# Three stretches of a fused attention and GELU kernel with their instructions put in another order

## The chip, the cores and the metric

The kernel runs on one core of a Trainium2 chip. The metric is the device time of one execution in microseconds (us). The engines work side by side, each through its own queue in order: TensorE (PE; its weight loads are listed apart as PEld), VectorE (DVE), ScalarE (ACT), GpSimd (POOL) and SyncE (SP), which issues the DMAs.

## The reference

A polynomial-sketch attention makes x, and a two-layer block with exact GELU is applied to x. Everything is float32 in the end (some inputs arrive as 64-bit words, and the kernel makes float32 of them itself).

```python
# q, k, v: (4, 4, 1088, 32); S1, S2: (8, 32); w_in: (128, 2048); w_out: (2048, 128)
def phi(x):
    a = np.einsum('rd,bhsd->bhsr', S1, x)
    b = np.einsum('rd,bhsd->bhsr', S2, x)
    return np.einsum('bhsi,bhsj->bhsij', a, b).reshape(*x.shape[:-1], r * r)
q_p, k_p = (phi(q), phi(k))
kv = np.einsum('bhsf,bhsd->bhfd', k_p, v)
z = np.sum(k_p, axis=2)
num = np.einsum('bhsf,bhfd->bhsd', q_p, kv)
den = np.einsum('bhsf,bhf->bhs', q_p, z)[..., None] + 1e-06
attn = num / den
x = attn.transpose(0, 2, 1, 3).reshape(B * S, H * D)      # 4352 tokens x 128
h = x @ w_in
g = 0.5 * h * (1.0 + erf(h / sqrt(2)))
out = g @ w_out
```

## The kernel before

**Tiles.** The 1088 tokens of each of the 4 batches are cut into two chunks of 512 and a rest of 64. That gives 8 main chunks (n = 0 to 7, two for each batch) and a ninth, the remainder, that holds the rests of all four batches, 256 tokens wide. For each chunk an x of 128 channels by tokens (xT) is made, and then 16 blocks (fi) of 128 hidden channels are gone through: `hidden(n, fi)` multiplies w_in by xT into a PSUM bank (L683) and ScalarE applies GELU (L690). For chunks 0 and 1 the first 8 blocks go through `project` (L818), an ordinary product with w_out that adds up in one PSUM bank. All other main blocks go through `two_products` (L767), a Strassen-like scheme in which GpSimd makes sums of GELU outputs (`token_sums`, L732 to L735) and seven products replace eight. The remainder goes through `project` with tokens as the output's rows (L815).

**Order.** It is written out by hand: at the end of the kernel every instruction is tied behind the one before it on its engine, in the order of the text. Steps t run over (n, fi); at each step come `drain`, then `hidden`, then the lists `slots[t]`, `done[t]` and `products[t]`. The lists hold small pieces of other work that are due at that step: keys and queries of the next batches, weights, the products of blocks whose GELU is done. The products of step (n, fi) are due two steps later (LAG = 2). Step 128 is the remainder's first.

**Prologue.** Before the first step, the keys of batch 0 are turned by TensorE (L333), multiplied with the sketch matrices (L373) and spread into features; key-value sums follow (L417, L423), then the numerators and denominators by token of chunk 0 (`numerators_by_token`, L635). `keep_busy` (L848) puts matmuls of zeros ahead of all this: 3 of 256 columns at the start, one of 128 columns later. A float32 matmul goes through TensorE in two passes, so each shows as two records.

**From numerator to x.** `divide` (L642) does three things on VectorE: it adds 1e-6 to the denominators (L650), takes the reciprocal (L651) and multiplies (L656) into x_tok, tokens by channels. For chunk 0 this is done in two halves of the tokens, the first with its products in two banks h_ps, the second in two banks o_ps. `turn_half` (L660) turns 256 tokens by two transposes on TensorE (L664) into a PSUM bank, and a copy (L665) brings it to xT: the first half by ScalarE, the second by VectorE. `first_hidden` (L697) then does the first hidden product by halves of the tokens.

**Chunk 1** goes the same way at step t = 3, beside chunk 0's first hidden blocks: numerators (L635, 64 records), `divide` in one piece, then the products `project(0, 0)` and `project(0, 1)`, and at step t = 4 the two turns with their copies, the first half of the first hidden product, `project(0, 2)`, and the second half.

**Weights** arrive as 64-bit words and become float32 in several short instructions (`Rounding`): low words (L260) and exponents (L279) on ScalarE, fields (L268, L273), mantissas (L287), signs (L292) and the product (L297) on VectorE. For the second piece of w_out, which `project(0, 2)` is the first to read, the mantissas are made by ScalarE and GpSimd (L284, L285); its product L297 on VectorE stands between chunk 1's division and the copy of chunk 1's second half. GpSimd goes on from L285 to `spread_sketches` (L468 to L478), small operations and copies.

**The remainder** gets its x at the end of step 127 by `attend` (L617) with a copy by ScalarE (L623); `products[128]` are four of the products of chunk 7's third block.

Of the kernel before, what the change touches and what calls it, by code (L numbers as in the profile page):

```python
# [8 lines left out]
FP = mybir.dt.float32  # L9
U32 = mybir.dt.uint32  # L10
AX = mybir.AluOpType
ACT = mybir.ActivationFunctionType
# [4 lines left out]
def kernel(  # L17
# [18 lines left out]
    pe, dve, act, pool, sp = nc.tensor, nc.vector, nc.scalar, nc.gpsimd, nc.sync  # L36
    B, H, S, D = q.shape
# [4 lines left out]
    NF = d_ff // 128  # L42
    NP = H // 2
# [3 lines left out]
    JC = 4  # L47
# [3 lines left out]
    C = D + 1  # L51
    LAG = 2
    NMAIN = B * NCH
# [7 lines left out]
    att = ctx.enter_context(tc.tile_pool(name="att", bufs=2))  # L61
# [9 lines left out]
    def work_bank():  # L71
        return work_banks()[:, 0]
# [11 lines left out]
    by_act, by_dve, by_pool = act.copy, dve.tensor_copy, pool.tensor_copy  # L84
# [10 lines left out]
    w_out_sb = [big.tile([128, c1 - c0], FP, name=f"w_out{i}") for i, (c0, c1) in enumerate(pieces)]  # L95
# [428 lines left out]
    def expand_products(n):  # L524


        W = width[n]
        for i in range(2):
            B_of[n, i] = work_banks()
        for s in range(2):  # L530
            for g in range(G):
                for c in range(NP):
                    rows = slice(g * D, (g + 1) * D)
                    pe.matmul(B_of[n, g // 2][c * F:(c + 1) * F, g % 2, s * W // 2:(s + 1) * W // 2],  # L534
                              lhsT=Srep[rows, s].rearrange("p i j -> p (i j)"),
                              rhs=qT[n][rows, 2 * c:2 * c + 2].rearrange("p r j t -> p r (j t)"), start=True, stop=True)
        qp[n] = att.tile([128, 2, CW], FP, name="q_pT")
# [89 lines left out]
    def numerators_by_token(n, banks, tokens):  # L627

        for at, i in enumerate(tokens):
            for r in range(2):  # L630
                for half in range(2):
                    for c in range(NP):
                        rows, col, tok = slice(c * F, (c + 1) * F), (at * 2 + r) * C, i * 128 + half * 64
                        v_at = r * 2 * D
                        pe.matmul(banks[c][half * 64:(half + 1) * 64, col:col + C], lhsT=qp[n][rows, r, tok:tok + 64],  # L635
                                  rhs=kz[0][rows, v_at:v_at + C], start=True, stop=True)
# [2 lines left out]
        x_tok[n, i] = att.tile([128, 2, H, D], FP, name=f"x_tok{i}", bufs=1)  # L639
        return x_tok[n, i]  # L640

    def divide(n, banks, tokens, by_head_pair):  # L642

        g = len(tokens) * 2
        den = att.tile([128, NP, JC * 2], FP, name="den_tok")[:, :, :g]
        parts = [slice(c, c + 1) for c in range(NP)] if by_head_pair else [slice(0, NP)]
        nd = [(banks[c.start][:, None] if by_head_pair else banks)[:, :, :g * C].rearrange("p b (g c) -> p b g c", c=C)
              for c in parts]
        for c, x in zip(parts, nd):
            dve.tensor_scalar(out=den[:, c], in0=x[:, :, :, D], scalar1=1e-6, scalar2=None, op0=AX.add)  # L650
        dve.reciprocal(out=den, in_=den)  # L651
        for i in range(len(tokens) // 2):
            to = x_half(n, tokens[0] // 2 + i).rearrange("p j (c r) d -> p c j r d", c=NP)
            for c, x in zip(parts, nd):
                for b in range(c.stop - c.start):
                    dve.tensor_mul(out=to[:, c.start + b], in0=x[:, b, i * 4:i * 4 + 4, 0:D].rearrange("p (j r) d -> p j r d", r=2),  # L656
                                   in1=den[:, c.start + b, i * 4:i * 4 + 4].rearrange("p (j r) -> p j r", r=2)[:, :, :, None]
                                   .broadcast_to([128, 2, 2, D]))

    def turn_half(n, i, ps, copy):  # L660
        if i == 0:
            xT[n] = att.tile([128, CW], FP, name="xT", bufs=3)
        for j in range(2):
            pe.transpose(ps[:, j * 128:(j + 1) * 128], in_=x_tok[n, i][:, j].rearrange("p h d -> p (h d)"), identity=ident)  # L664
        copy(out=xT[n][:, i * 256:(i + 1) * 256], in_=ps[:, :256])  # L665


    g_of, o_of = {}, {}

    def w_tile(w, fi):  # L670
        i = max(i for i, (c0, c1) in enumerate(pieces) if c0 <= fi * 128)
        at = fi * 128 - CUTS[i]
        return w[i][:, at:at + 128]
# [98 lines left out]
    def drain(n):  # L772


        C, N = (att.tile([128, 2, CW], FP, name="sums") for i in range(2))
        lo, hi, one, two = slice(0, 64), slice(64, 128), slice(0, HW), slice(HW, CW)
        a0, a1 = acc[n]

        act.copy(out=C[lo, 0], in_=a1[hi])
        act.copy(out=N[hi, 0, one], in_=C[lo, 0, one])  # L780

        dve.tensor_copy(out=N[lo, 0, one], in_=a0[lo, one])  # L782
        dve.tensor_add(out=C[lo, 1], in0=a1[lo], in1=C[lo, 0])
        dve.tensor_add(out=N[lo, 1, one], in0=a0[lo, two], in1=N[lo, 0, one])
        for half in (lo, hi):
            dve.tensor_add(out=C[half, 0, one], in0=a0[lo, one], in1=C[lo, 1, two])
        dve.tensor_add(out=C[hi, 0, two], in0=a0[hi, two], in1=C[hi, 0, one])
        dve.tensor_add(out=N[hi, 1, one], in0=a0[hi, one], in1=C[hi, 0, two])
        drained[n] = C, N
# [14 lines left out]
            dve.tensor_add(out=N[:, 1], in0=N[:, 1], in1=usual[n])  # L804
        return N[:, 1]

    def project(n, fi, parts=range(B // 2)):
        first, final = fi == 0, fi == (USUAL if n < NCH else NF) - 1
        if first:
            o_of[n] = out_bank() if n < NMAIN else [work_bank() for i in range(B // 2)]  # L810
        g = g_of[n, fi]
        if n == NMAIN:

            for i in parts:
                pe.matmul(o_of[n][i][:, :128], lhsT=g[:, i * 128:(i + 1) * 128], rhs=w_tile(w_out_sb, fi),  # L815
                          start=first, stop=final)
            return
        pe.matmul(o_of[n], lhsT=w_tile(w_out_sb, fi), rhs=g, start=first, stop=final)  # L818

    def store(n):  # L820
        oT = mlp.tile([128, JC, d_model], FP, name="oT")
# [23 lines left out]
    def keep_busy(n, ps, cols=256):  # L845
        for i in range(n):
            noughts = [nc.const_aps.tensor(0.0, [128, m], FP) for m in (128, cols)]
            pe.matmul(ps[:, CW - cols:], lhsT=noughts[0], rhs=noughts[1], start=True, stop=True)  # L848

    bank = work_bank()  # L850
    keep_busy(3, bank)
    r = Rounding(SR)
    r.low_words()
    r.fields()
# [10 lines left out]
    banks = [out_bank(), out_bank()]  # L865
# [28 lines left out]
    by_act(**late[0])  # L894
    w_in[1].low_words()
    w_in[1].exponent_fields()
    w_in[1].exponents()
    parts = [range(2), range(2, JC)]
    nd = [[hidden_bank(), hidden_bank()], [out_bank(), out_bank()]]
    for banks, tokens in zip(nd, parts):  # L900
        numerators_by_token(0, banks, tokens)
    expand_products(1)
    for banks, tokens in zip(nd, parts):
        divide(0, banks, tokens, by_head_pair=True)
    w_in[1].mantissa_fields()
    turn_half(0, 0, hidden_bank(), by_act)
    turn_half(0, 1, hidden_bank(), by_dve)
# [175 lines left out]
    for t in range(len(steps) + LAG):  # L1083
        if t < 4:

            hidden(0, t)
            if t == 1:
                w_out[0].low_words()
                w_out[0].exponents()
                w_out[0].finish()  # L1090
                w_out[1].fields()
            if t == 2:
                w_out[1].low_words()
            if t == 3:
                banks = work_banks()
                numerators_by_token(1, halves(banks), range(JC))
                w_out[1].mantissas(by_pool=True)
                w_out[1].exponents()
                divide(1, banks, range(JC), by_head_pair=False)
                w_out[1].signs()  # L1100
                w_out[1].product()
                for u in range(4):
                    for f, *a in products[u]:
                        f(*a)
            continue
        if t == 4:
            for i, copy in enumerate((by_act, by_dve)):
                turn_half(1, i, work_bank(), copy)
            first_hidden(1, 0)
            for f, *a in products[t]:  # L1110
                f(*a)
            first_hidden(1, 1)
        for n in drains[t]:
            drain(n)
        if t < len(steps):
            n, fi = steps[t]
            hidden(n, fi, by_halves=t >= 18 and (n < NMAIN or fi < 5))
        if t < len(steps) and steps[t][0] < NMAIN and steps[t][1] % NB == NB - 1:
            n, b = steps[t][0], steps[t][1] // NB
            if b >= first_block(n):  # L1120
                token_sums(n, b)
        for f in slots[t]:
            f()
        for n in done[t]:
            store(n)
        if t != 4:
            for f, *a in products[t]:
                f(*a)
    for n in done[len(steps) + LAG]:
# [40 lines left out]
```

## Time and profile before

| | |
|---|---|
| median of 3 runs | 261.31 us (261.14 to 261.8) |
| profiled execution, its own time | 263.36 us |
| its span, first to last instruction | 261.6 us |
| instructions | 5751 |
| DMA | 13.48 MB, mean 52 GB/s |
| hidden products L683, all | 137.3 us busy in 514 records |
| block products L767, the largest group | 57.5 us busy in 224 records |
| GELU on ScalarE L690 | 73.0 us busy in 128 records |
| sums on GpSimd L732 to L735 | some 36 us each, 28 records each |
| output products L818 | 16.3 us busy in 32 records |

The profile holds one execution of the program, with the start and the length of each instruction. A row such as "L683 PE MATMUL h_ps<-xT,w_in" names the line of the code, the engine, the operation, and which tile is made from which. The matmuls are pipelined: a row's length holds the time that the last results need to leave the array, so the starts of neighbours, and not the lengths, tell how fast they follow each other. Idle time of an engine is put down to the instruction whose semaphore came last.

### The profile page before, as it was taken

How to read it: one execution, taken by the hardware profiler on the slowest of the kernel's cores; microseconds unless marked ns; L12 is line 12 of the kernel's file. 1: busy time of each engine (PE TensorE's matmuls, PEld its weight loads, DVE VectorE, ACT ScalarE, POOL GpSimd, SP SyncE). 2: the span in 40 equal slices, each digit the busy share in tenths (PEclk: the TensorE clock that was granted, in tenths of full speed). 3: DMA queues.
4: the chain of work that ended last, by engine and by line, in shares of the span. 5: the costliest groups of instructions: out<-in, count | busy, mean ns of one | idle time of the engine just before them, and what ended most of it. 6: DMA issues, size and time to landing. Idle time of an engine off the chain costs nothing.

```text
span 261.6 us, 5751 instructions
## 1 busy us (share of the span) xinstructions
PE 256.9 (98%) x2331; PEld 134.7 (51%) x2331; DVE 151.4 (58%) x315; ACT 114.8 (44%) x219; POOL 163.8 (63%) x173
## 2 busy tenths in 40 slices
PE   8999999999999999999999999999999999999994
PEld 6755444344454554444444454444445444445794
DVE  2687678977789997690087957540565043600330
ACT  3465767442535333353335333523453334334441
POOL 3313004799978875687758767787768776877200
PEclk9999999999999999999999999999999999999999
DMA  6449848721000201102000001010001100010020
GB/s 203 136 143 358 218 111 212 217 70 15 0 3 5 33 6 23 20 3 40 3 0 3 0 16 27 4 31 10 3 0 21 21 4 0 12 31 0 3 40 20
DMA packets 29530, 13.48 MB, mean 52 GB/s; under 512 B 21824, under 2 KB 27712, under 8 KB 29504
## 3 DMA queue, kind: packets, MB, share of 16 engines
q1 hardware_dynamic: 29472, 13.12, 20.2%
q8 instruction: 18, 0.29, 0.5%
q14 instruction: 8, 0.07, 0.1%
q10 hardware_dynamic: 32, 0.00, 0.0%
HBM read 10.88 MB, written 2.23 MB: 50 GB/s over the span
## 4 chain that ended last, share of the span: by engine, by line
PE 97%; DVE 1%; issue 0%; ACT 0%
PE h_ps L683 44%; PE o_ps L767 33%; PE o_ps L818 5%; PE w_ps L815 3%; PE w_ps L428 1%; PE w_ps L617 1%; PE w_ps L568 1%; PE w_ps L848 1%; PE h_ps L697 1%; PE h_ps L333 1%; PE o_ps L417 1%; PE w_ps L534 1%; PE w_ps L934 1%; PE w_ps L635 0%; PE o_ps L373 0%; DVE x_tok L656 0%
## 5 line engine op out<-in xcount | busy, mean ns | idle before, releaser
L683 PE MATMUL h_ps<-xT,w_in 128*64 128x512 f32 (+3 forms) x514 | 137.3, 576 | 0.0
L690 ACT ACTIVATE block<-h_ps 128x512 f32<-128x512 f32 (+1 forms) x128 | 73.0, 571 | 120.5 <-PE h_ps L683 120.1
L767 PE MATMUL o_ps<-block,w_out 128*64 128x256 f32 x224 | 57.5, 379 | 0.0
L683 PEld LDWEIGHTS h_ps<-xT,w_in 128*64 128x64 f32 (+1 forms) x514 | 41.8, 142 | 29.5 <-issue 11.6
L732 POOL TENSOR_TENSOR bits_low<-block 128x512 f32<-128x512 f32 x28 | 35.7, 1274 | 27.5 <-ACT block L690 27.5
L767 PEld LDWEIGHTS o_ps<-block,w_out 128*64 128x64 f32 x224 | 30.5, 137 | 37.5 <-issue 26.7
L733 POOL TENSOR_TENSOR bits_a<-block 128x512 f32<-128x512 f32 x28 | 35.9, 1284 | 12.8 <-ACT block L690 12.8
L734 POOL TENSOR_TENSOR bits_e<-bits_a,block 128x512 f32<-128x512 f32 x28 | 36.1, 1289 | 2.2
L735 POOL TENSOR_TENSOR bits_m<-block,bits_e 128x512 f32<-128x512 f32 x28 | 35.8, 1280 | 2.2
L580 DVE STREAM_TRANSPOSE w_ps<-w_ps 128x512 f32<-128x512 f32 (+1 forms) x7 | 4.9, 693 | 42.7 <-PE w_ps L568 30.0
L767 PE MATMUL o_ps<-block,small 128*64 128x256 f32 x112 | 29.0, 381 | 0.0
L767 PE MATMUL o_ps<-bits_low,small 128*64 128x256 f32 x112 | 29.0, 381 | 0.0
L767 PE MATMUL o_ps<-bits_a,small 128*64 128x256 f32 x112 | 28.8, 379 | 0.0
L767 PE MATMUL o_ps<-bits_m,w_out 128*64 128x256 f32 x112 | 28.7, 379 | 0.0
L767 PEld LDWEIGHTS o_ps<-block,small 128*64 128x64 f32 x112 | 14.9, 137 | 17.7 <-issue 10.1
L782 DVE COPY sums<-o_ps 64x256 f32<-64x256 f32 x8 | 3.3, 417 | 34.6 <-PE o_ps L767 34.6
L767 PE MATMUL o_ps<-bits_e,small 128*64 128x256 f32 x112 | 17.2, 384 | 0.0
L818 PE MATMUL o_ps<-g,w_out 128*128 128x512 f32 x32 | 16.3, 597 | 0.0
L767 PEld LDWEIGHTS o_ps<-bits_m,w_out 128*64 128x64 f32 x112 | 15.3, 137 | 0.0
L767 PEld LDWEIGHTS o_ps<-bits_a,small 128*64 128x64 f32 x112 | 15.2, 137 | 0.0
L767 PEld LDWEIGHTS o_ps<-bits_low,small 128*64 128x64 f32 x112 | 14.9, 137 | 0.0
L767 PEld LDWEIGHTS o_ps<-bits_e,small 128*64 128x64 f32 x112 | 7.5, 136 | 10.6 <-issue 9.1
(181 smaller groups left out, 304.8 us busy)
## 6 DMA issues: line engine op xcount, KB each, us to landing
out_dram<-oT SPq DMA_DIRECT2D x26, 64.0 KB, 2.2
block<-in_moe_w_in_dram SPq DMA_DIRECT2D x3, 512.0 KB, 6.8
block<-in_moe_w_out_dram SPq DMA_DIRECT2D x3, 512.0 KB, 12.3
k<-in_k_dram SPq DMA_DIRECT2D x12, 128.0 KB, 2.8
v<-in_v_dram SPq DMA_DIRECT2D x12, 128.0 KB, 3.3
q<-in_q_dram SPq DMA_DIRECT2D x24, 64.0 KB, 2.2
k<-in_k_dram SPq DMA_DIRECT2D x2, 256.0 KB, 2.9
q<-in_q_dram SPq DMA_DIRECT2D x2, 256.0 KB, 3.8
```

Source lines behind the costliest of these rows:

```text
L333: pe.transpose(ps[:, i * 128:(i + 1) * 128], in_=s, identity=ident)
L580: dve.transpose(out=tok, in_=ps[:, :, :H2])
L683: pe.matmul(ps[rows, :W], lhsT=w[:, rows], rhs=xT[n][:, :W], start=True, stop=True)
L690: act.activation(out=g_of[n, fi][:, :W], in_=ps[:, :W], func=ACT.Gelu)
L732: pool.tensor_sub(out=s[3], in0=a11, in1=a21)
L733: pool.tensor_add(out=s[1], in0=a21, in1=a22)
L734: pool.tensor_sub(out=s[2], in0=s[1], in1=a11)
L735: pool.tensor_sub(out=s[4], in0=a12, in1=s[2])
L767: pe.matmul(acc[n][bank][half * 64:(half + 1) * 64, col:col + HW], lhsT=fixed, rhs=moving, start=opens and e == 0 and name in "4715", stop ...
L782: dve.tensor_copy(out=N[lo, 0, one], in_=a0[lo, one])
L815: pe.matmul(o_of[n][i][:, :128], lhsT=g[:, i * 128:(i + 1) * 128], rhs=w_tile(w_out_sb, fi), start=first, stop=final)
L818: pe.matmul(o_of[n], lhsT=w_tile(w_out_sb, fi), rhs=g, start=first, stop=final)
```

## The change

It has four edits.

1. For the second half of chunk 0's tokens, the addition of 1e-6 moves from VectorE (two L650) to ScalarE: a new function `denominators` does two activations with a bias into the same kind of tile, and `divide` takes it as given. On ScalarE they stand ahead of the exponents (L279) of the second piece of w_in, which move behind them.
2. At step 3, `project(0, 1)` is cut into two halves of its columns, and the two turns of chunk 1 move ahead from step 4 to stand one behind each half; the order of the copies on ScalarE and VectorE stays.
3. At step 128 the list `products[128]` comes ahead of the remainder's first `hidden`.
4. At the start, a fourth `keep_busy` matmul of 64 columns is put behind the three of 256.

```diff
-    def divide(n, banks, tokens, by_head_pair):
+    def divide(n, banks, tokens, by_head_pair, den=None):
         g = len(tokens) * 2
-        den = att.tile([128, NP, JC * 2], FP, name="den_tok")[:, :, :g]
+        given = den is not None
+        if not given:
+            den = att.tile([128, NP, JC * 2], FP, name="den_tok")[:, :, :g]
...
-        for c, x in zip(parts, nd):
+        for c, x in zip(parts, nd) if not given else ():
             dve.tensor_scalar(out=den[:, c], in0=x[:, :, :, D], scalar1=1e-6, scalar2=None, op0=AX.add)
         dve.reciprocal(out=den, in_=den)
...
+    def denominators(banks):
+
+        den = att.tile([128, NP, JC * 2], FP, name="den_tok")[:, :, :JC]
+        for c, ps in enumerate(banks):
+            act.activation(out=den[:, c], in_=ps[:, :JC * C].rearrange("p (g c) -> p g c", c=C)[:, :, D], func=ACT.Copy, bias=1e-6)
+        return den
...
-    def project(n, fi, parts=range(B // 2)):
+    def project(n, fi, parts=range(B // 2), cols=slice(None)):
...
-        pe.matmul(o_of[n], lhsT=w_tile(w_out_sb, fi), rhs=g, start=first, stop=final)
+        pe.matmul(o_of[n][:, cols], lhsT=w_tile(w_out_sb, fi), rhs=g[:, cols], start=first, stop=final)
...
     keep_busy(3, bank)
+    keep_busy(1, bank, 64)
...
     w_in[1].exponent_fields()
-    w_in[1].exponents()
...
         numerators_by_token(0, banks, tokens)
+    den = denominators(nd[1])
+    w_in[1].exponents()
     expand_products(1)
-    for banks, tokens in zip(nd, parts):
-        divide(0, banks, tokens, by_head_pair=True)
+    for banks, tokens, by in zip(nd, parts, (None, den)):
+        divide(0, banks, tokens, by_head_pair=True, den=by)
...
                 w_out[1].product()
-                for u in range(4):
-                    for f, *a in products[u]:
-                        f(*a)
+                project(0, 0)
+                project(0, 1, cols=slice(0, 256))
+                turn_half(1, 0, work_bank(), by_act)
+                project(0, 1, cols=slice(256, 512))
+                turn_half(1, 1, work_bank(), by_dve)
             continue
         if t == 4:
-            for i, copy in enumerate((by_act, by_dve)):
-                turn_half(1, i, work_bank(), copy)
             first_hidden(1, 0)
...
         for n in drains[t]:
             drain(n)
+        sooner = t == NMAIN * NF
+        if sooner:
+            for f, *a in products[t]:
+                f(*a)
...
-        if t != 4:
+        if t != 4 and not sooner:
             for f, *a in products[t]:
                 f(*a)
```

## The prediction

> **What bounds the kernel now.** I read the page first, then what TensorE waited for, then the chain of waits from 13.7 to 26.5 us, then the timelines of single engines at the three places that the change touches.
>
> Of the page, the busy row and the chain by engine; of the waits of TensorE, the last two (us in total, times, longest):
>
> ```profile
> PE 256.9 (98%) x2331; PEld 134.7 (51%) x2331; DVE 151.4 (58%) x315; ACT 114.8 (44%) x219; POOL 163.8 (63%) x173
> ...
> PE 97%; DVE 1%; issue 0%; ACT 0%
> ...
> PE h_ps L697 <- ACT xT L665: 0.2, 1, 0.2
> PE h_ps L664 <- DVE x_tok L656: 0.2, 1, 0.2
> ```
>
> Of the chain, the pieces around the first two places (start, length, what):
>
> ```profile
> 15.45 0.15 DVE den_tok L650 x2
> 15.60 0.02 issue
> 15.62 0.21 DVE den_tok L651
> 15.83 0.02 issue
> 15.86 0.50 DVE x_tok L656 x2
> 16.36 0.14 issue
> 16.49 0.41 PE h_ps L664 x2
> ...
> 21.86 1.91 PE o_ps L818 x4
> 23.77 0.23 PE w_ps L664 x2
> 24.00 0.02 issue
> 24.03 0.38 ACT xT L665
> ```
>
> Of the timelines of GpSimd, VectorE, TensorE and ScalarE, the rows that decide the second and the third place:
>
> ```profile
> 23.87 0.24 POOL L476 TENSOR_TENSOR S_ab<-sT,own_r 128x32 f32<-128x32 f32 x1
> ...
> 24.15 0.42 DVE L297 TENSOR_TENSOR w_out<-bits_m,bits_e 128x256 f32<-128x256 f32 x1 [0.52 <-POOL S_ab L476]
> ...
> 239.12 0.65 PE L767 MATMUL o_ps<-bits_e,small 128*64 128x256 f32 x4
> 239.78 0.65 PE L683 MATMUL h_ps<-xT,w_in 128*64 128x256 f32 x4
> ...
> 239.34 0.39 ACT L623 COPY xT<-w_ps 128x256 f32<-128x256 f32 x1
> ```
>
> TensorE holds 98% of the span and 97% of the chain that ended last, so only TensorE time that is removed, or a hole in TensorE's row that is closed, can move the end. Only two waits of 0.2 us are booked to it, but a busy matmul here includes its drain, so holes must be read from start-to-start distances. Three are left. Near 16.3 us TensorE stands until VectorE has divided the second half of chunk 0. Near 24.2 us it stands until ScalarE has copied chunk 1's first turned half. Near 239.7 us it stands until ScalarE has copied the remainder's x (239.34 + 0.39 = 239.73). Everything between is dense. Where I say that a matmul streams from a time, it is the row's start, plus up to 0.1 us when its weight load had to wait (its row is then that much longer than its fellows'), or the next start less its own pass.
>
> **What the Trainium skill says.** "SBUF — State Buffer", section "SBUF: two separate sides": VectorE, with two SBUF inputs, and GpSimd share one port pair under an exclusive lock, held for a whole instruction. The trace agrees: the product L297 is behind no late operand (bits_m was ready at 22.35 + 0.72 = 23.07), yet it starts 0.04 us after GpSimd's S_ab ends (24.11). "TensorE: Matmul & The Clock Gate", Part 1: the array starts at half clock, and a free-running window of about 3.4 us with enough activity releases it. The trace agrees on two speeds: the 32 matmuls of L534 take 2.01 us at 8.28 and 1.12 us at 14.80. "ScalarE: Activation LUTs", "What ACT_TABLE_LOAD costs": an activation with immediate scale and bias costs 186 ns + 0.833 ns per column.
>
> **The change, part by part.** Times below are those of the profiled execution of before.
>
> *Epsilon by ScalarE.* It removes two L650 from VectorE; the reciprocal L651 that followed at 15.62 can start where they did, at 15.36, if ScalarE's denominators are there. They need the products L635, whose last ends at 14.22 + 0.65 = 14.87. Two activations of 4 columns are 0.19 us each by the skill's price; the nearest row is the pair of 128x64 copies L389, 0.33 us for both. So they are done at about 14.92 + 0.33 = 15.25, just in time (0.1 us to spare). Queued behind them on ScalarE is the exponents' L279 (0.51), which moves from 14.66 to about 15.2 and ends at 15.7. ScalarE then idled 1.16 us until its copy L665 at 16.32, so this is hidden; L279's reader on VectorE, L292, starts only at 17.61. The second x_tok is then done 0.26 us earlier, at 16.09 instead of 16.35, and the second turn L664 starts at 16.23 instead of 16.49. That is not all gain: the first L697 stays at 16.84, since it waits for ScalarE's copy of the FIRST half (16.32 + 0.37 = 16.69). The gain shows at the second pair of L697. Two passes of 256 columns hold TensorE 2 x 0.215 = 0.43 us (512 columns, one pass: 0.43). The first pair's stream ends at 17.13 + 0.215 = 17.35. The second pair ran 17.52 to 17.95, waiting for VectorE's copy, which ended at 17.36. After the change that copy starts at 16.68 (turn done 16.65) and ends at 17.11, so the pair follows at 17.35 and ends at 17.78. **Gain 0.17 us.** What is late next is the first GELU: it waits for these very products, so the chain behind it moves along whole. If the denominators are late, the gain falls to zero, and 0.1 us of loss is the worst I see.
>
> *Chunk 1's turn amid the output products.* Before: L818 twice (4 passes of 0.43, streaming 21.89 to 23.61), four turns L664 (0.11 each, to 24.04), a stand until ScalarE's copy ends at 24.40, and L697 streaming at 24.56. The second product is now cut in column halves and the turns put between. It costs no TensorE columns, and the extra weight loads (0.19) hide beside matmuls of 0.215. New times: product (0,0) to 22.75, first half of (0,1) to 23.18, turn of half 0 to 23.40 (its x_tok is ready at 22.92), second half to 23.83, turn of half 1 to 24.04. Before, L697 streamed 0.84 us after the start of the last turn of half 0 (23.72 to 24.56); that start is now 23.29, so L697 streams at 24.13 and is done at 24.56 instead of 24.99: 0.43 us gained up to here. But the next is product (0,2), whose weights are made by that L297 on VectorE, which ends at 24.15 + 0.42 = 24.58. Before it was not late (its matmul started at 24.99). Now it is: with 0.04 us of semaphore and 0.11 us of a load that is not prefetched it streams at 24.74, not 24.56. GpSimd's run of small operations that hold the port starts from ScalarE's L284, which follows TensorE, and moves with it, so the order of the lock stays. **Gain 24.99 - 24.74 = 0.25 us**; between 0.25 and 0.43 us if the lock falls otherwise. VectorE's copy of half 1 (24.50 to 24.92) stays ahead of its use at 25.60.
>
> *Last block products ahead of the remainder's first hidden.* The four passes of L767 on bits_e stream from 239.17 to 239.60 (two run side by side, 0.216 a pair); L683 streams at 239.83, after the copy. The hole is 0.23 us. The eight L767 records now put first take four pairs, 0.86 us; their bits_m was made long before (GpSimd's row at 235.77). L683 then starts at 240.46, when xT has been ready for 0.7 us. **Gain 0.23 us.** The remainder's first GELU comes 0.6 us later against its neighbours, but the next user of its bank is the third hidden product, behind 0.43 us of L683 and 0.86 us of L767, against 0.6 us that the GELU needs: hidden.
>
> *One more filler matmul at the start.* L848 with 64 columns is two passes at half clock, 2 x 0.107 = 0.21 us (from 0.21 for 128 columns at 4.60). The six before stream until 3.46, and the first turn L333 starts at 3.72, when k has landed (issued at 0.73, 2.9 us to landing: 3.63). It fills 3.46 to 3.68: **cost zero**, 0.2 us if k lands sooner in other executions.
>
> No DMA is moved, SP's and POOL's queues keep their order. The sum is 0.17 + 0.25 + 0.23 = 0.65 us. The profiled execution took 263.36 us with a span of 261.6; I expect a span of 260.9 and 262.7 us for it. The median of the runs is 261.31, 2.05 below the profiled one; the same subtraction gives **260.65 us**, 0.25% less. A measurement of this kernel tells about 0.3% (0.78 us) from no change, so the likeliest outcome is a gain just too small to be told.
>
> **The rivals.** (a) L297 isn't late, because VectorE gets the port ahead of GpSimd's S_ab or L474: all 0.43 us, 0.83 us in sum, 260.5. For it: one wait at a lock between engines with rough spans. Against it: L292 ends at 23.64, after GpSimd's run has begun at 23.40. (b) The clock. The filler raises activity in a window in which the array is still at half speed; if that window now counts, full clock comes 3.4 us sooner and up to half of that, 1.7 us, is saved, less what VectorE then holds back (k_p ends only at 9.1 us): 259.5. Against it: turns and small matmuls fill most of that stretch, and 0.2 us of 3.4 is little. (c) Slower: the same window goes the other way. With the window running free of the kernel's start, moving the start of the first turns can leave its activity under the mark, and full clock comes 3.4 us later. That half-speed stretch costs 1.7 us, less 0.65: 262.35. It decides from a rise that is 1.3 us later (half of it, 0.65, eats the gain), and can be told from about 2.9 us on. For it: the rise came only about 10 us in, so earlier windows did fail; against: nothing takes matmuls out of the window. (d) Parts do nothing, as the filler costs 0.2 us or the denominators are late: 0.2 to 0.35 us left to gain, about 261.0.
>
> **How the numbers follow.** Main case 0.53, own range 260.3 to 261.0 from the runs' spread of 0.3 us; (a) 0.15; (b) 0.08; (c) 0.09; (d) 0.15. The bound of 0.3% lies at 260.53. Faster takes a third of the main case (0.18), most of (a) (0.11), and (b) (0.08): 0.37. Slower is (c): 0.09. The rest, 0.54, is within 0.3%. The range of 8 in 10 runs from 259.9 to 261.5: it leaves out most of (b) and (c).
>
> **What would show it.** Right: the second pair of L697 directly behind the first; no idle time ahead of the turn of half 1 of chunk 0; product (0,2) of chunk 0 starting 0.04 us behind the end of VectorE's L297, still with a wait for S_ab; L683's first remainder product without a wait for L623; L333 starting at 3.7. Wrong: a reciprocal waiting for ScalarE; a first L333 later than 3.75; the 32 matmuls of L534 near 8.3 us taking clearly more or less than 2.0 us, which would mean that the clock rose at another time and would swamp all three gains.

## The result, and the profile after

The changed kernel took 260.65 us (median of 7 runs, 260.29 us the fastest). One of the seven took 514.69 us at a granted clock of 0.90; the ratio below leaves it out, and without it the median would be 260.53 us. The kernel before, run beside it on the same chip, took 261.61 us. The ratio is 0.9966 with a 95% interval of [0.9953, 0.998], a gain of 0.9 us, or 0.5 to 1.2 us by the interval. The interval leaves out 1, so there is a gain, where the prediction held one too small to be told for the likeliest outcome. That the forecast of 260.65 us is met to the hundredth is luck: it was taken from a median of 261.31 us and held a gain of 0.66 us (and 260.53 us would not have met it). What was forecast too small, and what stood for nothing in the sum, has to be found in the trace.

The profiled execution took 260.86 us with a span of 259.1 us. Of its page, the busy row and the chain by engine, and what TensorE waited for (us in total, times, longest):

```profile
PE 254.6 (98%) x2335; PEld 134.8 (52%) x2335; DVE 151.6 (59%) x313; ACT 114.9 (44%) x221; POOL 163.5 (63%) x173
...
PE 98%; ACT 0%; issue 0%; DVE 0%
```

```profile
PE w_ps L857 <- PEq L1169: 0.8, 1, 0.8
PE h_ps L706 <- ACT xT L674: 0.2, 1, 0.2
```

TensorE's busy time fell by 2.3 us, more than the change can remove. The wait for VectorE's x_tok is gone; the wait for ScalarE's copy of the first turned half has stayed, as the prediction's working for this place had it.

The chain of waits of the changed kernel around the first two places (start, length, what; L673 is now the turn, L706 the first hidden products, L827 the output products):

```profile
13.24 1.05 PE w_ps L534 x32
14.29 0.38 PE h_ps L673 x2
14.67 0.02 issue
14.70 0.38 ACT xT L674
15.08 0.14 issue
15.21 1.10 PE h_ps L706 x4
...
20.05 1.49 PE o_ps L827 x4
21.54 0.22 PE w_ps L673 x2
21.76 0.43 PE o_ps L827 x2
22.19 0.22 PE w_ps L673 x2
22.41 0.51 PE h_ps L706 x2
22.92 0.86 PE o_ps L827 x2
```

VectorE's five pieces (addition, reciprocal, multiplication) are gone from the chain at the first place. At the second the chain stays on TensorE from the first output product to the product (0,2) at 22.92, with no ScalarE copy and no piece of VectorE in it: the standstill at chunk 1's turn is closed without a new one.

The rows of VectorE, and of TensorE and ScalarE near the remainder's first hidden product, in the timelines of the changed kernel (start, length, what):

```profile
21.42 0.41 DVE L292 SCALAR_TENSOR_TENSOR bits_e<-small,bits_r 128x256 uint32<-128x256 uint32 x1
21.94 0.45 DVE L297 TENSOR_TENSOR w_out<-bits_m,bits_e 128x256 f32<-128x256 f32 x1
22.45 0.42 DVE L674 COPY xT<-w_ps 128x256 f32<-128x256 f32 x1
...
236.85 0.65 PE L776 MATMUL o_ps<-bits_e,small 128*64 128x256 f32 x4
...
238.20 1.03 PE L692 MATMUL h_ps<-xT,w_in 128*64 128x256 f32 x8
...
237.08 0.39 ACT L623 COPY xT<-w_ps 128x256 f32<-128x256 f32 x1
```

L692 starts 0.73 us after the copy that it needs (237.08 + 0.39 = 237.47): the third hole is closed. And L297, which the prediction held to be late, follows L292 after 0.11 us; in the kernel before it stood 0.52 us. That is the surprise of this profile.

To weigh the places apart from the start of the kernel, the table cuts each execution at TensorE's own instructions. Stage A goes from the first numerator product L635 of chunk 0 to that of chunk 1, stage B from there to chunk 1's first 512-column hidden product, stage D from chunk 7's first L617 (at 211.74 us in the kernel before) to the remainder's first output product (L815, now L824); the expectation of e1 calls that L617 the remainder's. "Stand" is the time from the end of chunk 1's L292 to the start of its L297. All are single profiled executions; where nothing that bears on a stage was changed, its length repeats to 0.01 us, but for A in e1 and e10, of which the last section tells.

| kernel | first L635 at | A | B | D | stand | ratio to before, 95% interval |
|---|---|---|---|---|---|---|
| before | 13.73 | 6.985 | 5.556 | 34.772 | 0.52 | |
| changed | 12.11 | 6.811 | 5.130 | 34.537 | 0.11 | 0.9966 [0.9953, 0.998] |
| before again (e1) | 12.17 | 8.006 | 5.556 | 34.774 | 0.52 | 1.0006 [0.9995, 1.0017] |
| filler alone (e2) | 12.11 | 6.985 | 5.555 | 34.776 | 0.51 | 1.0002 [0.999, 1.0014] |
| changed without filler (e3) | 11.52 | 6.809 | 5.129 | 34.536 | 0.10 | 0.9971 [0.9959, 0.9983] |
| turn of chunk 1 alone (e4) | 11.65 | 6.987 | 5.313 | 34.777 | 0.53 | 0.9991 [0.9981, 1.0] |
| epsilon alone (e5) | 11.71 | 6.807 | 5.557 | 34.772 | 0.11 | 0.9988 [0.9974, 1.0003] |
| e4, GpSimd's sketches earlier (e6) | 11.67 | 6.977 | 5.306 | 34.771 | 0.52 | 0.9989 [0.9976, 1.0002] |
| changed, long GpSimd sum (e7) | 11.92 | 6.810 | 5.530 | 34.535 | 0.10 | 0.9983 [0.9974, 0.9992] |
| changed, half turned early (e8) | 11.54 | 7.302 | 5.130 | 34.536 | 0.10 | 0.9978 [0.9966, 0.999] |
| changed, two VectorE more (e9) | 11.86 | 6.809 | 5.310 | 34.537 | 0.52 | 0.9973 [0.9958, 0.9987] |
| e4, two VectorE fewer (e10) | 11.76 | 7.309 | 5.130 | 34.774 | 0.10 | 0.9995 [0.9976, 1.0015] |
| changed again (e11) | 11.61 | 6.808 | 5.130 | 34.536 | 0.10 | 0.9962 [0.9947, 0.9976] |
| e4, four VectorE more (e12) | 12.18 | 6.985 | 5.129 | 34.777 | 0.10 | one run: no ratio |

The change takes 0.174 us from A, 0.426 us from B and 0.235 us from D: 0.835 us. The other 1.6 us by which its span is shorter lie ahead of the first L635 (13.73 against 12.11 us), and there the kernel before, profiled once more, stands at 12.17. They are not the change's.

### The profile page after: what moved, and what is told of

Same layout as the page of the kernel before. It is cut to its first block, busy times and chain, and to the rows that moved or that the text cites. A ratio compares the mean times of both kernels' runs of the same rounds, so it can differ in the third digit from the quotient of the medians.

```text
span 259.1 us, 5758 instructions
## 1 busy us (share of the span) xinstructions
PE 254.6 (98%) x2335; PEld 134.8 (52%) x2335; DVE 151.6 (59%) x313; ACT 114.9 (44%) x221; POOL 163.5 (63%) x173
## 4 chain that ended last, share of the span: by engine, by line
PE 98%; ACT 0%; issue 0%; DVE 0%
PE h_ps L692 45%; PE o_ps L776 33%; PE o_ps L827 5%; PE w_ps L824 3%; PE w_ps L428 2%; PE w_ps L857 1%; PE w_ps L617 1%; PE w_ps L568 1%; PE o_ps L417 1%; PE w_ps L534 1%; PE h_ps L706 1%; PE h_ps L333 1%; PE w_ps L945 1%; PE w_ps L635 0%; PE w_ps L333 0%; PE h_ps L373 0%
## 5 line engine op out<-in xcount | busy, mean ns | idle before, releaser
L692 PE MATMUL h_ps<-xT,w_in 128*64 128x512 f32 (+3 forms) x514 | 137.1, 576 | 0.0
L692 PEld LDWEIGHTS h_ps<-xT,w_in 128*64 128x64 f32 (+1 forms) x514 | 41.9, 142 | 29.2 <-issue 11.6
L827 PE MATMUL o_ps<-g,w_out 128*128 128x512 f32 (+1 forms) x34 | 16.5, 572 | 0.0
```

What stands on the lines that cost most here:

```text
L692: pe.matmul(ps[rows, :W], lhsT=w[:, rows], rhs=xT[n][:, :W], start=True, stop=True)
L827: pe.matmul(o_of[n][:, cols], lhsT=w_tile(w_out_sb, fi), rhs=g[:, cols], start=first, stop=final)
```

## The experiments

**Is the shorter start the filler's doing?** e1 is the kernel before, unchanged. e2 is the kernel before with the filler (edit 4), e3 the changed kernel without it.

> The kernel before, unchanged, for a second trace. Theory 'phase' (the array's clock rises at a moment that is not tied to the kernel): its rise will not stand at 10.2 us again but anywhere from about 4 to 10 us, the prologue up to the first L635 of chunk 0 will take between 12 and 13.7 us, and the three stages behind it keep their lengths: first L635 of chunk 0 to first L635 of chunk 1 6.98 us, from there to chunk 1's first L683 5.56 us, first L617 of the remainder to first L815 34.77 less nothing, all within 0.03. Rival 'filler' (without the added filler matmul the rise comes late): rise at 10.2 us again, first L635 at 13.7. Time ratio 1.000 +- 0.001 in both.

> The kernel before with the fourth filler matmul alone. Theory 'phase': ratio 1.000 +- 0.001 (0 to +0.2 us), stages as in before, rise anywhere. Rival 'filler': rise at 5.9 us as in the changed kernel's profile and ratio 0.993 to 0.996, as the late rise cost the profiled execution of before 1.6 us.

> The changed kernel without the filler. Theory 'phase': the same time as the changed kernel, ratio to before 0.9968 (0.17 + 0.43 + 0.23 = 0.83 us), with stages 6.81, 5.13 (or 5.31 when GpSimd holds the port against L297) and 34.54 us. Rival 'filler': the whole or half of the gain is gone, ratio 0.998 to 1.000, with a rise at about 10 us.

The start is read from the 32 products L534 near 8 us. In the kernel before they took 2.01 us at half clock. In the timelines of the changed kernel they and the first turns read

```profile
0.78 3.22 PE L857 MATMUL w_ps<-const-float32-0.0 128*128 128x256 f32 x8 [0.78 <-PEq L1169]
3.79 1.06 PE L333 MATMUL h_ps<-ident,k 128*128 128x128 f32 x4
...
7.54 1.12 PE L534 MATMUL w_ps<-qT,Srep 32*64 32x256 f32 x32
```

so the clock had risen earlier. By the granted clock in the traces it rose at 10.21 us after the start in the kernel before and at 5.86 us in the changed one. But it rose at 6.35 us in e1 (no filler), at 5.87 us in e2 (filler) and at 4.63 us in e3 (no filler), and in all fourteen executions at 3.68 to 10.21 us with no order by the filler: 3.68 to 5.87 us with it (six executions), 3.69 to 10.21 us without it (eight). Timed over many runs, e2 is at 1.0002 of before, and e3 at 0.9971 against the changed kernel's 0.9966. The filler does nothing that these runs can tell. The single profile of before had caught a late rise. The Trainium skill ("TensorE: Matmul & The Clock Gate", Part 1) has the window of about 3.4 us run freely of the program. Thirteen of the fourteen rises lie within 2.7 us (3.68 to 6.36), less than one such window, and before's stands 3.9 us behind the last of them. That fits a free phase, with one window more in that execution; why it took one more, no run shows.

The filler's place did cost a little: L333 starts at 3.76 to 3.79 us wherever the filler is, and at 3.54 to 3.72 us wherever it isn't. In twelve of the other thirteen executions k lands sooner (3.41 to 3.52 us) than in the profile of before (3.58 us), so the gap that the filler was to fill was mostly shorter than that profile showed.

**Which edit closes which hole?** e4 is the kernel before with the turn of chunk 1 alone (edit 2), e5 the kernel before with the epsilon by ScalarE alone (edit 1).

> The kernel before with chunk 1's turn moved alone. If the moved turn fills the hole by itself, the stage from chunk 1's first L635 to its first L683 is 5.13 us when L297 gets the port early, and 5.31 us when it is held until S_ab ends (the prediction's case); the other two stages stay at 6.98 and 34.77. If the 5.13 us needed the epsilon edit too (through a shift of VectorE against GpSimd), it is 5.31. Ratio 0.9984 or 0.9990.

> The epsilon edit alone. Theory 'VectorE pulls GpSimd ahead': VectorE gains 0.26 us on its own chain but TensorE only 0.17, so the fields of w_out's second piece (L273) and, through ScalarE's L284, GpSimd's run from L285 on start about 0.09 us earlier against chunk 1's first L635 (1.54 instead of 1.63 us behind it); L297 then follows L292 by about 0.10 us as in the changed kernel, not by 0.52 us as in before. The stage from chunk 0's first L635 to chunk 1's is 6.81 us, the next one stays at 5.56 since nothing waits for L297 there, the last stays at 34.77. Rival (the lock's order is chance): L297 follows by 0.5 us in this kernel. Ratio 0.9993 in both.

e5 gives A = 6.807 us, the whole 0.18 us there, and nothing in B. e4 gives B = 5.313 us, a gain of 0.243 us, and nothing in A. D moves in neither, nor with the filler alone (e2), so its gain is left to edit 3, which was not run by itself. A's gain and D's stand by themselves, while B's 0.426 us is 0.24 us of the turn and 0.18 us that appears only when turn and epsilon edit are together. Yet the epsilon edit is 8 us away from that place. In e5 the stand is 0.11 us already; it pays nothing there, because without the earlier turn the product that needs L297 isn't waiting.

**Is it GpSimd's hold on the port?** That was the prediction's reading of the stand. e6 is e4 with GpSimd's sketch operations (L468 to L478, S_ab among them) put ahead of its L285, where they are over before 14.2 us (20.28 less 6.10 in the view below); e7 is the changed kernel with a GpSimd sum of 512 columns, whose result isn't used, put ahead of them, so that GpSimd is busy where L297 comes:

```diff
-    at(11, spread_sketches)
...
+                spread_sketches()
```

> Chunk 1's turn moved alone (as in e4), and GpSimd's spread_sketches moved ahead of its L285, so that GpSimd touches nothing while VectorE wants L292 and L297. Theory 'port': L297 follows L292 at once (0.1 us) and the second stage falls from 5.31 to 5.13 us. Rival (L297 waits in e4 for something else, an operand or VectorE itself): it stays at 5.31. Ratio 0.9984 against 0.9990.

```diff
+    hold = big.tile([128, CW], FP, name="hold")
...
+        some = main["v", 0][:, 0:2].rearrange("p h j d -> p (h j d)")
+        pool.tensor_add(out=hold, in0=some, in1=some)
```

> The changed kernel with one more GpSimd sum of 128x512, reading SBUF, put between L285 and L468; its result is not used. Theory 'port': VectorE's L292 and L297 are pushed behind it, some 0.8 to 1.4 us, the product (0,2) waits for L297, and the second stage grows from 5.13 to between 5.9 and 6.5 us; ratio 1.000 to 1.002, so the whole gain is gone. Rival (no lock, the two engines do not meet): 5.13 us, ratio 0.997.

The timelines of VectorE and GpSimd in e6:

```profile
21.15 0.41 DVE L292 SCALAR_TENSOR_TENSOR bits_e<-small,bits_r 128x256 uint32<-128x256 uint32 x1
22.08 0.43 DVE L297 TENSOR_TENSOR w_out<-bits_m,bits_e 128x256 f32<-128x256 f32 x1 [0.52 <-DVE bits_e L292]
...
20.28 0.72 POOL L285 TENSOR_TENSOR bits_m<-bits_high,bits_low 128x256 f32<-128x256 f32 x1 [6.10 <-ACT bits_high L284]
20.95 0.21 POOL L349 MEMSET v_rem_aug<- 128x128 f32 x1
```

GpSimd has nothing to do from 21.16 us until L297, and L297 still starts only at 22.08 us, with 0.52 us of stand. The trace now books it to L292, VectorE's own instruction before it. The lock as the cause of this stand falls, and with it the prediction's reading of the releaser in the profile of before: S_ab was only the last that had ended.

That says nothing against the lock itself. The Trainium skill ("SBUF — State Buffer", section "SBUF: two separate sides") has it held for a whole instruction, and e7 agrees:

```profile
21.23 1.05 DVE L292 SCALAR_TENSOR_TENSOR bits_e<-small,bits_r 128x256 uint32<-128x256 uint32 x1
22.38 0.42 DVE L297 TENSOR_TENSOR w_out<-bits_m,bits_e 128x256 f32<-128x256 f32 x1
...
20.95 1.04 POOL L471 TENSOR_TENSOR hold<-v 128x512 f32<-128x512 f32 x1
```

Beside GpSimd's sum of 1.04 us L292 takes 1.05 us instead of 0.41 us and ends 0.3 us after it. But here the held port shows as a LONGER instruction, not as idle time ahead of one, and L297 follows after 0.10 us. B grows to 5.530 us, by 0.40 us, less than the 0.8 us or more that was expected: the sum began before L292, which ends 0.64 us later than it would have, and L297 wasn't pushed any further.

**Is it a place in VectorE's program?** The stand goes with the kernels whose VectorE has two more instructions before it. Counted with semaphore instructions, chunk 1's L297 is VectorE's 65th in before, e1, e2, e4 and e6, all with the stand, and the 63rd in the changed kernel, e3, e5, e7 and e8, all without. (These numbers are those of the expectations; in the traces I count one fewer throughout, 64th and 62nd. The difference of two is what matters.) Two edits turn the count alone, each far from the place, in the 2.5 us at the start in which VectorE waits for its first load. e9 is the changed kernel with two instructions more:

```diff
     dve.memset(ones, 1.0)
+    dve.memset(ones, 1.0)
+    dve.memset(ones, 1.0)
```

> The changed kernel, with two more VectorE instructions at its very start (the memset of ones repeated twice, in the 2.5 us in which VectorE waits for the first load). In every kernel so far that showed the 0.5 us ahead of chunk 1's L297 this instruction was the 65th of VectorE's program (semaphore instructions counted), in every one that did not it was the 63rd, because the epsilon edit had taken two away. Theory place (the stall belongs to a place in VectorE's instruction stream, not to any partner of L297): L297 is the 65th again, starts 0.5 us after L292's end, and the stage from chunk 1's first L635 to its first 512-wide product takes 5.31 us, not 5.13; the other stages stay at 6.81 and 34.54; ratio 0.997 to 0.998. Rival moment (the epsilon edit, by moving the field instructions 0.09 us, takes L297 out of somebody's way): 0.10 us and 5.13 us as in the changed kernel.

e10 is e4 with two instructions moved to GpSimd:

```diff
     for t in v_aug:
-        dve.memset(t[:, :, :, D:C], 1.0)
+        pool.memset(t[:, :, :, D:C], 1.0)
```

> The turn of chunk 1 alone (epsilon and block products as in the kernel before), with the two L241 memsets at the start moved from VectorE to GpSimd, so that L297 of chunk 1 becomes VectorE's 63rd instruction without the epsilon edit. Theory place: L297 starts 0.10 us after L292's end and the stage takes 5.13 us, where the turn alone had 0.53 and 5.31; the stage before it stays 6.99 and the remainder's 34.78; ratio 0.998. Rival moment: 0.5 us and 5.31 us stay, since the field instructions stand where they stood; ratio 0.999.

> The changed kernel once more, beside the two. All theories: 6.81, 5.13 and 34.54 us for the three stages, L297 0.10 us after L292, ratio 0.997. If the rise of TensorE's clock is a matter of phase it falls anywhere from 3.7 to 10.2 us; if the filler fixes it, at 5.86 us as in the first profile.

VectorE's timeline in e9, where lines are shifted by two (L299 is the old L297):

```profile
21.17 0.41 DVE L294 SCALAR_TENSOR_TENSOR bits_e<-small,bits_r 128x256 uint32<-128x256 uint32 x1
22.11 0.42 DVE L299 TENSOR_TENSOR w_out<-bits_m,bits_e 128x256 f32<-128x256 f32 x1 [0.52 <-POOL S_ab L478]
```

and in e10:

```profile
21.57 0.41 DVE L292 SCALAR_TENSOR_TENSOR bits_e<-small,bits_r 128x256 uint32<-128x256 uint32 x1
22.09 0.45 DVE L297 TENSOR_TENSOR w_out<-bits_m,bits_e 128x256 f32<-128x256 f32 x1
```

Both ways, the count alone turns it. In e9 the stand is back at 0.52 us and B is 5.310 us although the epsilon edit is in; A and D keep their gains. In e10 the stand is gone and B is 5.130 us although the epsilon edit is not in. The changed kernel once more (e11) repeats its three stages to 0.003 us. The rival, that the epsilon edit moves the moment of L297, falls, and so does the theory under which e5's 0.11 us had been expected.

The ratios of e9 and e11, 0.9973 and 0.9962, lie in the right order, but 0.18 us is 0.07% and their intervals overlap; the stage lengths carry the verdict. e10's ratio of 0.9995 holds less of a gain than the 0.43 us of B, inside its interval; its profiled execution lost 0.3 us in A, of which more below.

e12 asked whether it is always the 65th. It is e4 with four repeated memsets in the place of e9's two: L297 becomes the 69th.

> The turn of chunk 1 alone, with the memset of ones repeated four times on VectorE, so that chunk 1's L297 is its 69th instruction and the third of the four multiplications of chunk 1's division is its 65th. If the stall sits at the 65th place, that third multiplication starts about 0.6 us after the second instead of 0.20, the work behind it on VectorE comes some 0.4 us later against TensorE, and L297 starts 0.10 us after L292. If the two instructions more or fewer mattered in another way than by the place, the four multiplications keep their 0.20 us and L297's delay is 0.5 or 0.1 us, one of the two values seen.

VectorE's timeline in e12 (lines shifted by two):

```profile
20.86 0.88 DVE L658 TENSOR_TENSOR x_tok<-w_ps,den_tok 128x128 f32<-128x128 f32 x4
21.66 0.41 DVE L294 SCALAR_TENSOR_TENSOR bits_e<-small,bits_r 128x256 uint32<-128x256 uint32 x1
22.18 0.45 DVE L299 TENSOR_TENSOR w_out<-bits_m,bits_e 128x256 f32<-128x256 f32 x1
```

The four multiplications, of which the third is the 65th now, come at 0.20 us one after the other, and the stand is gone, B 5.129 us. So L297 stands as the 65th and not as the 63rd or the 69th, but the 65th doesn't stand whatever it is. L297 as the 65th has one thing of its own: the instruction before it, the 64th, is a semaphore wait in VectorE's queue for L292. But it has that at every place. Two instructions more or fewer also shift the count of VectorE's own semaphore, which that wait reads; these runs don't tell the place from the count. Which of these the stand needs, and what VectorE does in that half microsecond, no run shows. No packet of the queues that bring instructions moves at that time in e4's trace (the nearest begins 0.4 us after L297's start), so a late load of instructions is not shown here.

**Can the last hole of A be closed?** After the change TensorE still waits 0.2 us for ScalarE's copy of the first half. e8 turns that half earlier, amid the expansion products, and has the sketches where e6 has them:

```diff
+                if s == 1 and g == 2:
+                    midway()
...
+    def half_0():
+        divide(0, nd[0], parts[0], by_head_pair=True)
+        turn_half(0, 0, hidden_bank(), by_act)
+
+    expand_products(1, half_0)
+    divide(0, nd[1], parts[1], by_head_pair=True, den=den)
```

> A version to beat both: the changed kernel with spread_sketches ahead of L285 (as in e6), and the turn of chunk 0's first half put amid chunk 1's L534, behind 12 of its 16 products, so that ScalarE's copy of it runs while the rest of L534 and the second turn do. In the changed kernel TensorE stands about 0.6 us between the last turn (14.66) and the first L706 (15.29). I expect the first stage to fall from 6.81 to 6.6 us, where VectorE's copy of the second half becomes the last to come, the second stage at 5.13, the third at 34.54; ratio 0.996. Rival: the first GELU waits for ScalarE's copies of L534's banks, and nothing is gained in the first stage.

It lost: A is 7.302 us against 6.811 us. TensorE's timeline of e8 (lines shifted by two):

```profile
12.60 1.09 PE L536 MATMUL w_ps<-qT,Srep 32*64 32x256 f32 x24
13.62 0.44 PE L675 MATMUL h_ps<-ident,x_tok 128*128 128x128 f32 x2
13.99 0.66 PE L536 MATMUL w_ps<-qT,Srep 32*64 32x256 f32 x8
14.58 0.44 PE L675 MATMUL h_ps<-ident,x_tok 128*128 128x128 f32 x2
14.86 1.38 PE L708 MATMUL h_ps<-xT,w_in 128*128 128x256 f32 x4
```

The expansion products are small tiles of 32 by 64 that start in groups, side by side. The starts of the single records in the traces tell what the split cost. In the changed kernel the 32 records start as four groups of eight, at 13.17, 13.44, 13.66 and 13.87 us. In e8 the first sixteen still make two groups of eight (12.60 and 12.87), but the cut falls in the middle of the other sixteen, and each part of these starts as two groups of four: at 13.08 and 13.30, then at 13.99 and 14.26 us. A group of four takes the same 0.22 us to the next as a group of eight, so two groups more are an estimated 0.43 us. One more passage from small products to a turn comes on top: it takes 0.32 us from the last group's start (13.30 to 13.62), where the next group would follow after 0.22. From the first product to the start of the last turn e8 needs 2.15 us (12.60 to 14.75), the changed kernel 1.57 us (13.17 to 14.74). Of these 0.58 us the closed hole gives back 0.09. A turn put between the two sixteens, where no group is broken, was not tried. No version here beats the changed kernel beyond the interval.

## Why the prediction was right, and where it was not

*Epsilon by ScalarE: right.* Predicted 0.17 us, measured 0.174 us in A, and 0.178 us when made alone. The denominators took 0.24 us for the pair, less than the 0.33 us taken from L389's row. ScalarE and VectorE in the changed kernel:

```profile
13.29 0.24 ACT L666 ACTIVATE den_tok<-o_ps 128x4 f32<-128x4 f32 x2 [0.16 <-PE o_ps L635]
13.42 0.51 ACT L279 ACTIVATE bits_r<-bits_e,below 128x256 uint32<-128x256 uint32 x1
...
13.73 0.19 DVE L653 RECIPROCAL den_tok<-den_tok 128x8 f32<-128x8 f32 x1
```

They end at 13.53 us, 0.2 us ahead of the reciprocal: in time, as worked out, and L279 behind them is hidden.

*Chunk 1's turn: the direction right, the size and the reason for the limit wrong.* Predicted 0.25 us in the main case, and 0.43 us if L297 were not late; measured 0.426 us. The step that failed is "GpSimd's run of small operations that hold the port starts from ScalarE's L284, which follows TensorE, and moves with it, so the order of the lock stays". It rests on the reading that L297 waits at the lock behind S_ab, and the lock isn't what stands there: with GpSimd idle the stand is the same 0.52 us (e6). Nor did the product (0,2) start right behind L297, as was to be seen if the prediction was right: in the changed kernel L297 ends at 22.39 us and the product starts at 22.92. The 0.25 us was not a bad estimate of the turn itself: with the stand left as it was, e4 measures 0.243 us and e9 0.246 us (5.556 less 5.310). The missing 0.18 us came from another edit by a way that no sum of durations contains: two VectorE instructions fewer ahead of L297 (e9, e10). Rival (a) had the right amount, 0.43 us, by the wrong cause.

*Last block products first: right.* Predicted 0.23 us, measured 0.235 us in D.

*The filler: right in the sum, wrong in its place.* It cost nothing measurable, but L333 does start up to 0.2 us later with it; the doubt written beside the "cost zero" was justified, and the prediction's sign of being wrong, a first L333 later than 3.75 us, did come up (3.79).

*The clock, rivals (b) and (c).* Neither happened as a consequence of the change, though another of the signs came up: the 32 products L534 took 1.12 us and not 2.0. They took 1.12 us in e1 too, which is the kernel before. The rise wanders by 6.5 us between executions of nearly one and the same program, and the profile of before had the latest rise of all fourteen. The working was safe from this because it compared stages behind the rise and subtracted the profiled execution's excess of 2.05 us as a constant. Read as a comparison of two spans, the same profiles would have shown 2.5 us of gain.

The stages give 0.835 us together; the prediction's sum was 0.65 us, and the timed gain of 0.9 us (0.5 to 1.2 us) cannot tell the two apart. All three parts gained, so rival (d) did not happen either.

## What to carry to other kernels

Compare two profiles of one kernel by stages between the dense engine's own instructions, not by spans: here gains of 0.17 to 0.43 us stood clear to 0.01 us beside a start that wandered by microseconds. A releaser named in a trace is the last thing that ended, not a cause; move it away before building a gain or a limit on it. And when an instruction stands without a late operand, shift it by a few instructions in its queue before looking for a partner on another engine. Before putting anything amid small products, look in which groups they start.

## What the runs showed of the hardware that I had not expected

VectorE can stand for 0.4 us more than usual (0.52 against 0.10 us) ahead of one instruction by the number of VectorE's instructions before it alone; two dummies of 0.1 us, 20 us earlier, bring the stand back. What of that number decides, the place or the semaphore's count, is open.

TensorE can do a like thing, and there a late load of instructions fits. In e1 it stands inside the products L635, between the 25th and 26th, in e10 at the very same one. The timeline of e1:

```profile
12.17 0.59 PE L635 MATMUL h_ps<-kz,q_pT 64*64 64x33 f32 x25
13.56 0.26 PE L635 MATMUL h_ps<-kz,q_pT 64*64 64x33 f32 x4 [0.80 <-issue]
```

"issue" says that the profile shows nothing it waited for. From start to start the hole is 1.02 us in e1 and 0.30 us in e10; elsewhere the largest distance in this row is 0.06 us. The traces also have the packets that bring instructions. The first of 16 KB on queue q8 (that it is TensorE's is inferred) landed at 12.37 us in e1 and TensorE went on 1.19 us later; in e10 it landed at 11.12 us and TensorE went on 1.31 us later. In the other twelve executions it landed at least 1.4 us before that product's start, and there was no hole. A block of instructions that lands late therefore fits all fourteen; that it is the cause was not tried.
